# Loading the first head pair's q and k in fp32 by the hardware queues, with the cast on chip

## The chip, the core and the metric

The kernel runs on one core of one Trainium2 chip. A core has five engines with an instruction stream each: TensorE (PE; its weight loads are listed apart as PEld), VectorE (DVE), ScalarE (ACT), GpSimd (POOL) and SyncE (SP). Transfers are issued from an engine's stream: here from POOL, SP and ACT. A transfer issued on POOL can change the type on its way (fp32 in DRAM to bf16 in SBUF); this kernel uses that for nearly all its loads. The metric is the device time of one execution in microseconds, the median over several runs.

## The reference

Two stages. First, an attention with "beacon" keys: 8 batches of 8 heads, 576 queries, and 16 + 576 keys of width 64. Query s may see all 16 beacons and the keys up to its own position:

```
k_all  = concat(beacon_k, k);  v_all = concat(beacon_v, v)
scores = q @ k_all^T / 8, masked causally for the 576 (not for the 16)
a      = softmax(scores);  attn = a @ v_all
```

The heads are then laid side by side into x of 4608 x 512, and a gated feed-forward follows:

```
out = (gelu(x @ w_gate) * (x @ w_val)) @ w_out        # 512 -> 1536 -> 512
```

All inputs and the output are fp32; the kernel computes in bf16 with fp32 sums.

## The kernel before

Per batch, q and k are brought into the form qkT: for each of four head pairs, width along the partitions (two heads of 64), positions along the columns. For the first two batches TensorE does the turning by transposes; later batches use transposing transfers. Scores of a pair are made in four chunks of columns (`CHUNKS`), each an exp on ScalarE into `exp_ring`; for batch 0 the causal mask is added on TensorE, by matmuls of `eye` (a shifted diagonal of ones) with `neg` (a staircase of large negative numbers), in `score_mms`. `attend` multiplies the exps with v, a column of ones gives the sums, `normalize` divides, and the result is turned into xT_sb. `gate_val` and `out_mms` are the feed-forward, run over chunks of 512 tokens and woven in between the attention of the next batch.

The order on each engine is the order in which the program is written: every operation goes through `keep`, which holds it in program order. Nothing is planned by costs. An engine waits only for the data and buffers of its next instruction, and what stands behind a waiting instruction on the same engine waits too.

At the start, which the change is about:

- SP issues the loads of batch 0's beacon keys and values in fp32, `kb_sb` and `vb_sb` (L474 to L477).
- POOL issues, through `load_qk6` (L120), the loads of batch 0's q and k by head pairs, cast to bf16 in flight, into the tile `qk6`: 96 partitions, of which each holds six consecutive positions of every head. Between the third and the fourth load POOL makes `eye` (L480). Loads of v, of the weights and of the next batches follow on the same stream.
- TensorE runs 66 small matmuls on zeros (`warm`, L228 and L519), whose result is not read.
- VectorE casts the two beacon tiles (L520, L521) and makes `neg` from `eye` by a running sum and a scaling (L522, L523).
- `transpose_both(0, 0)` (L223): `transpose_half` for k (12 transposes, and one of the beacon keys), copied out by VectorE (L217); `transpose_half` for q with `by_act`, which first runs eight transposes of zeros as fillers (L209) and then the twelve of q, copied out by ScalarE (L215). `beacon_part` (L221) copies the beacons' 16 columns.
- The first score chunks `c((0, 0))`, `c((0, 2))` follow, then the next pair's transposes, and so on.

Of the kernel before, what the change touches and what calls it, by code (L numbers as in the profile page):

```python
# [7 lines left out]
P = 128  # L8
B, H, S, NB, D = 8, 8, 576, 16, 64
SK = S + NB  # L10
N_TOK = B * S
D_MODEL = 512
# [30 lines left out]
FP32 = mybir.dt.float32  # L43
BF16 = mybir.dt.bfloat16
ACT = mybir.ActivationFunctionType
# [6 lines left out]
def kernel(  # L52
# [12 lines left out]
    nc = tc.nc  # L65
    keep = tc.keep_in_program_order
# [6 lines left out]
    opool = ctx.enter_context(tc.tile_pool(name="opool", bufs=2))  # L73
# [18 lines left out]
    q_ring, k_ring, v_ring = [], [], []  # L92
# [14 lines left out]
    def dma(out_ap, in_ap):  # L107
        keep(nc.gpsimd.dma_start(out=out_ap, in_=in_ap))  # L108

    qk6 = {}  # L110

    def qk6_of(b):
        if b not in qk6:
            qk6[b] = (
                hpool.tile([P, 2, H, 6 * D], BF16, name="qk6", tag="hT_sb"),
                npool.tile([NB, H, D], BF16, name="kb", tag="kb"),
            )
        return qk6[b]

    def load_qk6(b, h0, h1, ws=(1, 0)):  # L120
        for w in ws:
            src = (q, k)[w]
            dma(
                qk6_of(b)[0][0:96, w, h0:h1, :],
                src[b, h0:h1, :, :].rearrange("h (p r) d -> p h (r d)", r=6),
            )
# [44 lines left out]
    def mm(out_ap, lhsT, rhs, start, stop, **kw):  # L171
        keep(nc.tensor.matmul(out_ap, lhsT, rhs, start=start, stop=stop, **kw))  # L172

    def act(out_ap, in_ap, func, **kw):
        keep(nc.scalar.activation(out_ap, in_ap, func, **kw))  # L175
# [30 lines left out]
    def transpose_half(b, m, w, by_act=False):  # L206
        pool, tag = ((psum_o, "o"), (psum_t, "t"))[w]
        t_ps = pool.tile([P, 1024], BF16, name="t_ps", tag=tag)
        for _ in range(8 if by_act else 0):  # L209
            tr(t_ps[0:D, 640:768], idle[:, 0:D])  # L210
        tr_part(b, m, w, t_ps)
        out_ap = qkT[:, m, w, NB:SK].rearrange("p (t r) -> p t r", r=6)
        in_ap = t_ps[:, 0:S].rearrange("p (r t) -> p t r", r=6)
        if by_act:
            act(out_ap, in_ap, ACT.Copy)  # L215
        else:
            keep(nc.vector.tensor_copy(out_ap, in_ap))  # L217
        return t_ps

    def beacon_part(m, t_ps):  # L220
        keep(nc.vector.tensor_copy(qkT[:, m, 1, 0:NB], t_ps[:, S:SK]))  # L221

    def transpose_both(b, m):  # L223
        k_ps = transpose_half(b, m, 1)
        transpose_half(b, m, 0, by_act=m == 0)
        beacon_part(m, k_ps)

    def warm(n):  # L228
        w_ps = psum_s.tile([P, 2, 512], FP32, name="w_ps", tag="s")
        for j in range(n):  # L230
            mm(w_ps[:, 0, 0:D], idle[:, 0:P], idle[:, 0:D], True, True)
# [12 lines left out]
    def scores(b, *parts):  # L244
        s_ps = psum_s.tile([P, 2, 512], FP32, name="s_ps", tag="s")
        c0 = 0
        for m, c in parts:
            score_mms(b, m, c, s_ps[:, :, c0 : c0 + CHUNK_W[c]])
            c0 += CHUNK_W[c]
        (m, c), n = parts[0], len(parts)  # L250
        o, w = CHUNK_OFF[c], CHUNK_W[c]
        act(
            exp_ring[:, m : m + n, :, o : o + w].rearrange("p g h c -> p h g c"),
            s_ps[:, :, 0 : n * w].rearrange("p h (g c) -> p h g c", g=n),
            ACT.Exp,
            scale=QK_SCALE,
        )
        if b:
            for m, c in parts:
                masks(b, m, c)  # L260
# [200 lines left out]
    def out_mms(ci, u0, u1):  # L461
        for u in range(u0, u1):
# [8 lines left out]
                if ci >= N_CHUNKS - 2:  # L471
                    store(nc.sync)

    kb_sb = opool.tile([NB, H, D], FP32, name="kb_sb", tag="o_sb")  # L474
    keep(nc.sync.dma_start(out=kb_sb, in_=beacon_k[0].rearrange("h t d -> t h d")))
    vb_sb = opool.tile([NB, H, D], FP32, name="vb_sb", tag="o_sb")
    keep(nc.sync.dma_start(out=vb_sb, in_=beacon_v[0].rearrange("h t d -> t h d")))  # L477
    load_qk6(0, 0, 2)
    load_qk6(0, 2, 4, (1,))
    keep(  # L480
        nc.gpsimd.affine_select(
            out=eye,
            in_=eye,
# [31 lines left out]
    def c(*parts):  # L515
        scores(0, *parts)

    keep(nc.scalar.preload_act_table_set(SET_EXP))
    warm(66)  # L519
    keep(nc.vector.tensor_copy(qk6[0][1], kb_sb))  # L520
    keep(nc.vector.tensor_copy(v_ring[0][0:NB, 0, :, 0:D], vb_sb))  # L521
    keep(nc.vector.tensor_tensor_scan(neg, eye, idle, -1.0, ALU.add, ALU.add))  # L522
    keep(nc.vector.tensor_scalar_mul(neg, neg, -MASKED))  # L523
    transpose_both(0, 0)
    c((0, 0))
    c((0, 2))
    transpose_both(0, 1)
# [143 lines left out]
```

The softmax here doesn't subtract the row's maximum and nothing guards it: scores larger than these inputs give would overflow.

## Time and profile before

| | |
|---|---|
| Median of 7 runs | 369.71 us (368.66 to 371.42) |
| The profiled execution's own time | 369.48 us |
| Its span, first to last instruction | 367.7 us |
| PE busy | 357.5 us, 97% of the span |
| PEld busy | 183.1 us, 50% |
| DVE busy | 152.3 us, 41% |
| ACT busy | 188.1 us, 51% |
| POOL busy | 161.0 us, 44% |
| Read from HBM, written to it | 38.27 MB, 9.44 MB |
| Transfers issued on POOL (q0) | 104848 packets, 19.11 MB |

Busy shares are means over the whole span; the start, the only part that the change edits, is some 24 us of it. Matmuls are pipelined, so TensorE's 97% is not 97% of its peak. In the views, "out<-in" names the tiles by their names in the program, and the line is that of the helper that records the operation (L172 all matmuls, L180 all transposes, L175 all activations, L108 POOL's loads), so instructions are told apart by their tiles. "SPq", "ACTq" and "POOLq" are the instruction streams that issue transfers. Times in the views are microseconds from the first instruction, if not marked otherwise.

### The profile page before, as it was taken

To read this page: it belongs to the slowest core of one execution; us is meant where nothing else is said; L and a number is where in the kernel's file an instruction comes from. 1 tells how busy PE (TensorE), PEld (TensorE's weight loads), DVE (VectorE), ACT (ScalarE), POOL (GpSimd) and SP (SyncE) were. 2 spreads that over 40 slices of the span, in tenths; PEclk is the share of its full clock that TensorE was granted. 3 is DMA by queue.
4 is the path that set the end of the run, shared out by engine and by line. 5 is a ranking of instruction groups with operands and counts; after the bars stand their busy time and mean duration, and the time that the engine had idled before them with its cause. 6 is when DMAs were issued, how large, how long until landed. Compare 5 with 4: busy or idle time off the path is not lost.

```text
span 367.7 us, 7507 instructions
## 1 busy us (share of the span) xinstructions
PE 357.5 (97%) x3018; PEld 183.1 (50%) x3061; DVE 152.3 (41%) x277; ACT 188.1 (51%) x243; POOL 161.0 (44%) x288
## 2 busy tenths in 40 slices
PE   7899999999999999999999999999999999999996
PEld 7664445444554455444644464445544464444443
DVE  4544536343443335433534254434444253333332
ACT  3963488237923593349623891369334953321210
POOL 8934487484538352954376353836230430000000
PEclk9999999999999999999999999999999999999999
DMA  8999999799259953999399925992495051000112
GB/s 108 176 204 204 194 141 122 134 143 125 79 123 138 136 83 96 146 142 83 69 161 132 136 59 120 150 141 76 108 132 53 33 80 58 0 2 29 57 38 107
DMA packets 154900, 39.65 MB, mean 108 GB/s; under 512 B 141424, under 2 KB 150384, under 8 KB 154864
## 3 DMA queue, kind: packets, MB, share of 16 engines
q0 software_dynamic: 104848, 19.11, 70.1%
q1 hardware_dynamic: 48000, 16.38, 25.7%
q10 hardware_dynamic: 2016, 3.67, 3.2%
q8 instruction: 24, 0.39, 0.4%
q14 instruction: 12, 0.10, 0.1%
HBM read 38.27 MB, written 9.44 MB: 130 GB/s over the span
## 4 chain that ended last, share of the span: by engine, by line
PE 70%; DMA 13%; SPq 7%; DVE 3%; issue 2%; POOL 2%; ACT 0%; POOLq 0%; DVEq 0%
PE gv_ps L172 26%; PE o_ps L172 23%; DMA qkT<-k_sb 9%; PE x_ps L172 9%; PE s_ps L172 8%; SPq L238 6%; DMA q_sb<-in_q_dram 3%; PE t_ps L180 2%; POOL v_sb L108 2%; DMA xT_sb<-y_sb 1%; DVE qkT L217 1%; PE w_ps L172 1%; PE v_ps L172 1%; PE g_ps L172 1%; DVE y_sb L336 1%
## 5 line engine op out<-in xcount | busy, mean ns | idle before, releaser
L175 ACT ACTIVATE ge_sb<-gv_ps 128x512 bf16<-128x512 f32 x101 | 59.5, 597 | 144.7 <-PE gv_ps L172 142.7
L427 DVE TENSOR_TENSOR hT_sb<-gv_ps,ge_sb 128x512 bf16<-128x512 f32 x101 | 69.1, 691 | 115.6 <-ACT ge_sb L175 113.2
L172 PE MATMUL gv_ps<-xT_sb,wg_sb 128*128 128x512 bf16 x394 | 110.9, 379 | 0.5
L172 PE MATMUL gv_ps<-xT_sb,wv_sb 128*128 128x512 bf16 x401 | 110.9, 379 | 0.1
L175 ACT ACTIVATE expT<-s_ps 128x960 bf16<-128x960 f32 (+3 forms) x112 | 99.7, 966 | 8.4 <-PE s_ps L172 8.0
L172 PE MATMUL o_ps<-wo_sb,hT_sb 128*128 128x512 bf16 (+2 forms) x415 | 101.7, 373 | 1.4 <-issue 0.2
L298 POOL TENSOR_SCALAR_AFFINE_SELECT expT<-expT 128x256 bf16<-128x256 bf16 (+2 forms) x140 | 51.8, 387 | 63.8 <-ACT expT L175 60.3
L172 PEld LDWEIGHTS <-wv_sb 128*128 128x128 bf16 x432 | 42.3, 98 | 50.4
L172 PEld LDWEIGHTS <-wg_sb 128*128 128x128 bf16 x432 | 42.0, 98 | 50.5 <-DMA xT_sb<-y_sb 0.7
L172 PEld LDWEIGHTS <-hT_sb 128*128 128x128 bf16 x444 | 38.9, 97 | 42.3 <-DVE y_sb L336 3.1
L172 PEld LDWEIGHTS <-expT 128*128 128x128 bf16 (+1 forms) x960 | 33.5, 97 | 10.8 <-DVE y_sb L336 4.1
L172 PE MATMUL s_ps<-qkT 64*128 64x512 bf16 (+5 forms) x384 | 33.6, 281 | 3.7 <-DVE qkT L221 1.6
L172 PE MATMUL x_ps<-v_sb,expT 128*128 128x65 bf16 (+1 forms) x960 | 37.1, 193 | 0.0
L108 POOL DMA_DIRECT2D v_sb<-in_v_dram x40 | 33.7, 859 | 5.8 <-DMA wv_sb<-in_moe_w_val_dram 1.7
L446 DVE COPY o_sb<-o_ps 128x512 f32<-128x512 f32 (+2 forms) x37 | 25.0, 676 | 27.1 <-PE o_ps L172 26.0
L108 POOL DMA_DIRECT2D k_sb<-in_k_dram x30 | 25.3, 845 | 18.5 <-DMA q_sb<-in_q_dram 13.4
L336 DVE TENSOR_TENSOR y_sb<-x_ps,r_sb 128x320 bf16<-128x320 f32 (+1 forms) x47 | 28.8, 612 | 1.6
L334 DVE RECIPROCAL r_sb<-x_ps 128x5 f32<-128x5 f32 (+1 forms) x47 | 9.6, 204 | 47.0 <-PE x_ps L172 47.0
L108 POOL DMA_DIRECT2D q_sb<-in_q_dram x30 | 25.3, 884 | 3.5 <-DMA wo_sb<-in_moe_w_out_dram 3.5
L172 PEld LDWEIGHTS <-qkT 64*128 64x128 bf16 x384 | 14.4, 94 | 19.7 <-issue 11.2
L378 POOL COPY hold_sb<-xT_sb 128x2 bf16<-128x2 bf16 x6 | 1.1, 187 | 34.7 <-DMA xT_sb<-y_sb 34.7
L613 ACT ACT_TABLE_LOAD x7 | 9.0, 1283 | 0.1
(49 smaller groups left out, 120.0 us busy)
## 6 DMA issues: line engine op xcount, KB each, us to landing
out_dram<-o_sb SPq DMA_DIRECT2D x21, 256.0 KB, 2.4
out_dram<-o_sb ACTq DMA_DIRECT2D x14, 256.0 KB, 3.0
v_sb<-in_v_dram POOLq DMA_DIRECT2D x24, 128.0 KB, 6.3
q_sb<-in_q_dram POOLq DMA_DIRECT2D x24, 128.0 KB, 8.9
k_sb<-in_k_dram POOLq DMA_DIRECT2D x18, 128.0 KB, 7.9
wo_sb<-in_moe_w_out_dram POOLq DMA_DIRECT2D x3, 512.0 KB, 14.4
wg_sb<-in_moe_w_gate_dram POOLq DMA_DIRECT2D x2, 512.0 KB, 11.1
wv_sb<-in_moe_w_val_dram POOLq DMA_DIRECT2D x2, 512.0 KB, 12.8
```

The costliest lines, as they stand in the source:

```text
L108: keep(nc.gpsimd.dma_start(out=out_ap, in_=in_ap))
L172: keep(nc.tensor.matmul(out_ap, lhsT, rhs, start=start, stop=stop, **kw))
L175: keep(nc.scalar.activation(out_ap, in_ap, func, **kw))
L180: keep(nc.tensor.transpose(out_ap, in_ap, ident[0:n, 0:n]))
L217: keep(nc.vector.tensor_copy(out_ap, in_ap))
L238: nc.sync.dma_start_transpose(out=qkT[:, :, w, c + j * P : c + j * P + n], in_=src[0:n, j, :, :].rearrange("p h d -> p (h d)"),)
L298: nc.gpsimd.affine_select(out=d, in_=d, pattern=[[0, 2], [1, n]], compare_op=ALU.is_ge, fill=0.0, base=NB if t == 0 else 0, channel_multip ...
L334: keep(nc.vector.reciprocal(r, x[:, :, :, D:DV]))
L336: nc.vector.tensor_tensor(out=y_of[i][:, :, h0:h1, :].rearrange("p j b d -> p b j d"), in0=x[:, :, :, 0:D], in1=r.to_broadcast([P, h1 - h0 ...
L427: nc.vector.tensor_tensor(out=h_of[ci][:, fi, :], in0=gv_of.pop((ci, fi))[1], in1=ge_sb, op=ALU.mult)
L446: keep(nc.vector.tensor_copy(o_sb[:, ti, c0:c1], o_ps))
L613: keep(nc.scalar.preload_act_table_set(SET_GELU))
```

## The change

Four edits, all at the start of the program.

1. Heads 0 and 1 of q and k for batch 0 no longer come by POOL's casting loads. k is loaded by SP and q by ACT, each as the first transfer of that engine, in fp32, into two tiles `raw` of the pool that later holds the output tiles. The beacon tiles `kb_sb` and `vb_sb` become slices of `raw[1]` that lie beside k; their loads follow k on SP.
2. ScalarE casts k from `raw` into the tile `qk6` (96 x 768, fp32 to bf16), and VectorE casts q.
3. On VectorE `neg` is now made ahead of the casts (of the beacon keys, then of q); the cast of the beacon values moves behind `transpose_both(0, 0)`.
4. `warm` runs 56 matmuls instead of 66.

On POOL the load of k for heads 2 and 3 is now first, and `eye` second.

```diff
-    kb_sb = opool.tile([NB, H, D], FP32, name="kb_sb", tag="o_sb")
+    raw = [opool.tile([P, 4, D_MODEL], FP32, name="raw", tag="o_sb") for _ in range(2)]
+    raw0 = [raw[w][0:96, 0:2, 0 : 6 * D] for w in range(2)]
+    for w, engine in ((1, nc.sync), (0, nc.scalar)):
+        keep(
+            engine.dma_start(
+                out=raw0[w], in_=(q, k)[w][0, 0:2, :, :].rearrange("h (p r) d -> p h (r d)", r=6)
+            )
+        )
+    kb_sb, vb_sb = (raw[1][0:NB, g, :].rearrange("t (h d) -> t h d", h=H) for g in (2, 3))
     keep(nc.sync.dma_start(out=kb_sb, in_=beacon_k[0].rearrange("h t d -> t h d")))
-    vb_sb = opool.tile([NB, H, D], FP32, name="vb_sb", tag="o_sb")
     keep(nc.sync.dma_start(out=vb_sb, in_=beacon_v[0].rearrange("h t d -> t h d")))
-    load_qk6(0, 0, 2)
     load_qk6(0, 2, 4, (1,))
...
     keep(nc.scalar.preload_act_table_set(SET_EXP))
-    warm(66)
-    keep(nc.vector.tensor_copy(qk6[0][1], kb_sb))
-    keep(nc.vector.tensor_copy(v_ring[0][0:NB, 0, :, 0:D], vb_sb))
+    warm(56)
+    act(qk6[0][0][0:96, 1, 0:2, :], raw0[1], ACT.Copy)
     keep(nc.vector.tensor_tensor_scan(neg, eye, idle, -1.0, ALU.add, ALU.add))
     keep(nc.vector.tensor_scalar_mul(neg, neg, -MASKED))
+    keep(nc.vector.tensor_copy(qk6[0][1], kb_sb))
+    keep(nc.vector.tensor_copy(qk6[0][0][0:96, 0, 0:2, :], raw0[0]))
     transpose_both(0, 0)
+    keep(nc.vector.tensor_copy(v_ring[0][0:NB, 0, :, 0:D], vb_sb))
     c((0, 0))
```

## The prediction

> **What bounds the kernel now.** I read the windows view first, cut at the events of the start; its columns are stretch, length, busy us (instructions) of PE, PEld, DVE, ACT and POOL, granted clock, DMA share and GB/s.
>
> ```profile
> 13.07:15.61 2.54, 2.07 (x53) 1.47 (x53) 1.50 (x3) 2.54 (x4) 2.54 (x4) 1.00 2.02 173
> 23.90:367.70 343.80, 337.29 (x2573) 166.61 (x2613) 140.04 (x246) 171.79 (x224) 142.52 (x258) 1.00 0.97 104
> ```
>
> From 23.9 us to the end TensorE is busy 337.29 of 343.80 us, so whatever the change wins or loses must happen ahead of that and then moves the end one for one. The stretch before it is ScalarE's: its exps run without a gap. The timeline has start, duration, engine, line, operation and, in brackets, the idle time before it:
>
> ```profile
> 0.82 0.40 SPq L475 DMA_DIRECT2D kb_sb<-in_beacon_k_dram  x1
> 1.38 0.77 POOL L108 DMA_DIRECT2D qk<-in_k_dram  x1 [0.86 <-POOLq L655]
> 4.76 0.51 PEld L180 LDWEIGHTS <-qk 96*64 96x64 bf16 x12
> 5.39 0.19 PE L180 MATMUL t_ps<-eye,kb 16*128 16x16 bf16 x1
> 5.51 0.80 PE L180 MATMUL t_ps<-eye,idle 128*64 128x128 bf16 x6
> 5.62 0.76 DVE L217 COPY qkT<-t_ps 128x576 bf16<-128x576 bf16 x1 [0.71 <-PE t_ps L180]
> 6.72 0.65 ACT L175 ACTIVATE qkT<-t_ps 128x576 bf16<-128x576 bf16 x1 [4.63 <-PE t_ps L180]
> 7.42 0.39 PE L172 MATMUL s_ps<-qkT 64*128 64x512 bf16 x2 [0.75 <-ACT qkT L175]
> 7.93 6.31 ACT L175 ACTIVATE expT<-s_ps 128x1024 bf16<-128x1024 f32 x7 [0.55 <-PE s_ps L172]
> 8.10 0.31 PEld L180 LDWEIGHTS <-qk 96*64 96x64 bf16 x12
> 13.24 6.12 ACT L175 ACTIVATE expT<-s_ps 128x960 bf16<-128x960 f32 x7
> ```
>
> The exps fill ScalarE from 7.93 to 19.36 us. So the size of the change is the shift of that 7.93. The chain of waits says what leads to it:
>
> ```profile
> 1.13 3.70 PE w_ps L172 x66
> 4.84 1.86 PE t_ps L180 x29
> 6.72 0.66 ACT qkT L175
> 7.42 0.75 PE s_ps L172 x12
> ```
>
> Warm-up, transposes of k and q with eight fillers between, the cast-out of q^T, scores. Nothing here waits for a transfer in the open, as the DMA issues show (KB, us to landing):
>
> ```profile
> qk<-in_k_dram POOLq DMA_DIRECT2D x1, 144.0 KB, 3.3
> qk<-in_q_dram POOLq DMA_DIRECT2D x1, 144.0 KB, 3.2
> kb_sb<-in_beacon_k_dram SPq DMA_DIRECT2D x1, 32.0 KB, 2.0
> out_dram<-o_sb ACTq DMA_DIRECT2D x1, 256.0 KB, 2.0
> ```
>
> k lands at 1.38 + 3.3 = 4.68 us, just under the warm-up's end (4.77); q at 2.14 + 3.2 = 5.34, under the fillers that start at 5.51. The first twelve transposes of k load in 0.51 us, the same twelve of the next pair (8.10) in 0.31: TensorE starts at half clock. In single records the fillers follow each other 107 ns apart up to 6.04 and 56 ns from 6.14, so the clock doubled at about 6.13.
>
> **What the skill says.** (1) "DMA: Bandwidth & Descriptors", section Issuing engines are not separate DMA queues: all issuers share the same 16 engines, and issuing from several saves only issue time. The trace can't yet show two such loads side by side. (2) "TensorE: Matmul & The Clock Gate", Part 1: TensorE doubles its clock after a busy window of about 3.4 us that runs freely. The trace agrees in kind: work from 1.13, full clock at 6.13; the window before that one, had TensorE idle until 1.13 and didn't lift it. How busy is busy enough, neither says.
>
> **The change, part by part.** Its own sum is made against the profiled execution (369.48 us, of it span 367.7, so 1.8 around it); the median shown, 369.71, lies 0.2 higher, and I add that at the end.
>
> *Loads.* k goes out on SP at about 0.82, q on ACT at 0.81, instead of 1.38 and 2.14 on POOL. Each is 2 x 576 x 64 x 4 = 295 kB, 192 runs of 1536 B. An issue holds its queue 0.4 us (row L475). On ACT the table load (0.81, 1.28 us) slips to about 1.2, ending 2.5, before anything needs ScalarE; on SP the beacons slip 0.4. The beacon key's first bytes move at about 1.82, 1.0 us after issue. The 256 KB stores moved at some 360 GB/s (their packets took 0.74 us); that is the nearest row, in the other direction. Both loads start together and, sharing engines, end together: 590 kB / 360 GB/s = 1.6 us, so 3.4; POOL's next load (heads 2 and 3, whose first bytes come near 2.85 because it inherits the slot at 1.38) takes some share: +0.2; from last packet to semaphore about 0.3, as the beacon shows. Landing 3.9 us. Bounds: 2.9 if k were served first, 4.5 if both get half the rate after 2.85. I take 3.9.
>
> *Casts.* k on ScalarE, 96 x 768: rows of 1024 columns take 1049 ns and 832 take 914 on that engine; "ScalarE: Activation LUTs", What ACT_TABLE_LOAD costs, prices an activation at 186 ns + 0.833 ns per column, 826 ns. With semaphores: ready at 3.9 + 0.05 + 0.83 + 0.05 = 4.83. On VectorE the beacon cast is 0.41 us (row L520, 16 x 512). The q cast has 768 columns: 0.41 x 768/512 = 0.62 at most. The beacon key, behind k on SP, lands at about 4.1; cast to 4.55, q to 5.2. VectorE's next work, the copy of k^T, stood at 5.62: covered, with 0.4 to spare; without that cover each 0.1 us late delays k^T, beneath the fillers and q's transposes another 0.3. The q transposes stand behind the fillers, not behind 5.2.
>
> *Mask constants.* Scan 0.69 and scaling 0.23 move ahead of the casts; the diagonal pattern on POOL comes one issue (0.7) after 1.38, at 2.15, so they run 2.6 to 3.6, while VectorE waits for transfers. Their reader is the mask matmul at 7.64. The cast of the beacon values moves behind k^T's small copy, +0.41 on VectorE near 6.5; its next copy is at 8.69 and v is first read at 16.42. All three are nothing on the path.
>
> *POOL.* Two issues leave (0.77 + 0.65): all its later loads start up to 1.4 us earlier. Nothing waits for them: the loads of heads 2 and 3 landed by 7.7 for transposes at 8.1, and no later gap of TensorE ends on a load except 0.2 us once.
>
> *Warm-up.* 56 instead of 66 at 53.5 ns apart: TensorE is free at 4.77 - 0.54 = 4.23 and then waits until 4.83. The wait that the shorter warm-up opens falls on the cast of k: TensorE idles 0.6 us, and everything of the chain is queued behind.
>
> *Sum.* k's transposes start 4.85 against 4.77: +0.08. Fillers begin 5.59; with the clock doubling at 6.13, five go at 107 ns and three at 56, done 6.30 against 6.26: +0.04. From there on the stages are as before. Change 0.0, rounded; span 367.7, profiled time 369.5; with the 0.2, **369.7 us**, own range 369.1 to 370.4 (landing bounds below, and half of the spread of runs).
>
> **Rivals.**
> *A: the loads are quick.* If k lands by 3.3, TensorE goes on at 4.23. For it: the queue is empty before 2.85. But at half clock eight fillers take 0.86 and q's transposes 0.5, so ScalarE's copy starts at 6.53 instead of 6.72: 0.2 gained; were the clock's window to fall elsewhere, at most the 0.54 of the warm-up. 369.2 to 369.5. More than 0.3% (1.1 us) would need the exp stage itself to shrink; it has no gap to give.
> *B, the other side: the hole costs the clock.* Place: 4.23 to 4.85, inside the window from 2.7 to 6.13 that released the clock here. Busy share falls from 100% to 82%. The window before had 46% and wasn't enough; it decides if the threshold lies above 82% (a third of 46 to 100, or surely if transposes count less than matmuls). Price: one window more, to 9.5. Fillers done 6.45, q's transposes 7.15 (before 6.68), first scores 0.27 slower: exps begin 8.65 instead of 7.93, +0.7, and the second pair's transposes, 0.5 more on the way to VectorE's copies: +1.2, time 370.9. A second window adds about 1.1: 372.0.
> *C: the two loads crawl,* landing at 4.5 or beyond. Transposes at 5.45, +0.7 less what the clock gives back: +0.4 to +0.6, 370.2. Against it: the beacon load's 2.0 us shows a short fixed part.
>
> **How the numbers follow.** No change that matters 44%, A 20%, B 22% (near half of it past one window's price), C 10%, and 4% for something faster that I don't see. 0.3% is 1.1 us, about what a measurement of this kernel can tell from no change; the runs before spread from 368.66 to 371.42, which moves some of each case over a bound. Slower: most of B and a little of C, 0.23. Faster: the 4%, and tails of A by spread, 0.11. The rest is 0.66. The range reaches down below A's 369.2 by the spread of a median (0.5), and up over B's first window: 368.7 to 371.5, leaving out a second window and the unseen gain.
>
> **What would show it.** Right: SP's and ACT's issues at 0.8; ScalarE's cast of k starting 3.8 to 4.1 for 0.83; a hole of TensorE of about 0.6 us between w_ps and t_ps; first exp within 0.2 of 7.93; POOL's later issues 1.4 us earlier with no effect on TensorE. A: no hole. B: the second pair's twelve weight loads still take 0.51 us, first exp beyond 8.5. The prediction is wrong if loads issued on SP and ACT interleave differently from what I assume, or if the clock's window reacts to the hole.

## The result: slower by about 1%

The changed kernel took 373.47 us in the median (372.54 to 375.19, 12 runs), the kernel before, run beside it, 369.55 us (367.98 to 372.39, 31 runs). The ratio is 1.0108, with a 95% interval of 1.0091 to 1.0125: about 4.0 us slower, and outside the range of the prediction. The profiled execution took 373.18 us, of it span 371.5.

The windows view of the changed kernel, with the columns as before (stretch, length, busy us and instructions of PE, PEld, DVE, ACT, POOL, granted clock, DMA share, GB/s), cut where the clock records change, and once more at 27.30, 3.4 us behind the last cut of before:

```profile
...
3.83:7.24 3.41, 1.09 (x26) 0.82 (x24) 1.08 (x2) 0.84 (x1) 3.41 (x6) 1.00 1.26 195
7.24:17.48 10.24, 9.32 (x144) 6.60 (x143) 4.14 (x10) 6.54 (x8) 9.58 (x13) 0.50 1.80 179
...
27.30:371.50 344.20, 337.23 (x2573) 166.67 (x2613) 140.05 (x246) 171.82 (x224) 140.63 (x256) 1.00 0.95 102
```

The last row holds the same 2573 matmuls as the row of before from 23.90 us on, and is 344.20 us long instead of 343.80. So 3.4 of the 3.8 us that the span grew lie ahead of it. Two rows show how: from 3.83 to 7.24 TensorE is busy 1.09 of 3.41 us, and from 7.24 to 17.48 it works at half clock. (The clock column reads 1.00 also ahead of a trace's first clock record, so it says nothing of the time before 3.83.)

The chain of waits, start and duration:

```profile
0.82 4.71 DMA raw<-in_k_dram
5.54 0.85 ACT qk L175
6.44 0.45 PE t_ps L180 x12
...
```

Where the warm-up matmuls led to the transposes before, now the load of k does, and its cast. In the timeline, the idle time ahead of the first weight loads of k is the hole:

```profile
1.13 3.01 PE L172 MATMUL w_ps<-idle 128*128 128x64 bf16 x56 [1.13 <-DVE idle L80]
...
5.54 0.84 ACT L175 ACTIVATE qk<-raw 96x768 bf16<-96x768 f32 x1 [2.99 <-DMA raw<-in_k_dram]
...
6.44 0.31 PEld L180 LDWEIGHTS <-qk 96*64 96x64 bf16 x12 [2.41 <-ACT qk L175]
6.44 0.45 PE L180 MATMUL t_ps<-eye,qk 96*64 96x96 bf16 x12 [2.29 <-ACT qk L175]
...
9.91 1.86 ACT L175 ACTIVATE expT<-s_ps 128x1024 bf16<-128x1024 f32 x2 [0.83 <-PE s_ps L172]
...
10.35 0.51 PEld L180 LDWEIGHTS <-qk 96*64 96x64 bf16 x12
```

The first pair's twelve weight loads take 0.31 us and the second pair's, at 10.35, take 0.51: the reverse of before. In the clock records the clock was raised at 3.83 and lost at 7.24. Of the twelve executions six, this one among them, have a mean granted clock of 0.986, which is what three windows of 3.41 us at half clock make of 371.5 us; the others have 0.999 or 1.000. In those the clock was not lost once it had been raised, but a late first rise doesn't show in that figure (e10 below has 1.000 with its clock up at 16.71 us). Exps start at 9.91 instead of 7.93. The transfers from 0.5 to 3.5 us, first the GB/s in 40 equal slices of that stretch, then the issues (KB, us to landing):

```profile
GB/s 0 0 0 0 0 0 0 0 0 0 0 0 0 0 0 0 0 20 102 164 143 102 102 143 61 123 164 164 143 102 205 205 164 307 328 410 369 389 369 389
...
raw<-in_q_dram ACTq DMA_DIRECT2D x1, 288.0 KB, 5.0
raw<-in_k_dram SPq DMA_DIRECT2D x1, 288.0 KB, 4.7
qk<-in_k_dram POOLq DMA_DIRECT2D x2, 144.0 KB, 5.1
```

Both fp32 loads are late, and so are their neighbours: POOL's loads took 3.3 and 3.2 us before, and the beacon keys, 4.9 us here, had taken 2.0. Up to 2.97 us (33 slices of 0.075) no slice moved more than 205 GB/s.

Two suspects stand out, the late k and the lost clock. They come together here, so they had to be pulled apart.

### The profile page after: what moved, and what is told of

It is laid out like the page before. It is cut to its first block, busy times and chain, and to the rows that moved or that the text cites. A ratio compares the mean times of both kernels' runs of the same rounds, so it can differ in the third digit from the quotient of the medians.

```text
span 371.5 us, 7490 instructions
## 1 busy us (share of the span) xinstructions
PE 359.6 (97%) x3008; PEld 184.3 (50%) x3051; DVE 152.9 (41%) x278; ACT 189.1 (51%) x244; POOL 160.3 (43%) x286
## 4 chain that ended last, share of the span: by engine, by line
PE 68%; DMA 20%; POOL 5%; issue 3%; DVE 3%; SPq 0%; ACT 0%; POOLq 0%; DVEq 0%
PE gv_ps L172 26%; PE o_ps L172 21%; PE x_ps L172 9%; DMA qkT<-k_sb 8%; PE s_ps L172 8%; DMA q_sb<-in_q_dram 8%; POOL v_sb L108 4%; DMA xT_sb<-y_sb 3%; PE t_ps L180 2%; DMA raw<-in_k_dram 1%; POOL q_sb L108 1%; DVE qkT L217 1%; PE v_ps L172 1%; PE g_ps L172 1%; DVE y_sb L336 1%
## 5 line engine op out<-in xcount | busy, mean ns | idle before, releaser
L172 PE MATMUL s_ps<-qkT 64*128 64x512 bf16 (+5 forms) x384 | 35.3, 291 | 3.2 <-DMA qkT<-k_sb 0.8
L180 PE MATMUL t_ps<-eye,qk 96*64 96x96 bf16 x192 | 7.9, 232 | 2.3 <-ACT qk L175 2.3
```

Source lines behind the costliest of these rows:

```text
L180: keep(nc.tensor.transpose(out_ap, in_ap, ident[0:n, 0:n]))
```

## Experiments

The theory at the outset: the late landing opens the hole, the hole costs TensorE its clock, and each has a price of its own. Its rivals: only the late start counts, and the clock is a symptom; or only the clock counts. For each run two shifts are given: that of the first gelu on ScalarE (26.07 us before, 29.50 in the changed kernel), behind which TensorE is bound, and that of the median, taken as ratio less 1 times 369.6. Profiles are of one execution each, medians of several: the profiled execution had the longest time of its kernel in e1, e9 and e10 (373.14, 373.83 and 372.71 us) and the shortest in e2 and e11 (371.55 and 368.39), so a shift of the gelu and one of the median needn't agree. "Clock up" is when the trace's clock records show full speed for good; for e1, which has no such record, the weight loads of 6.26 stand in.

### Late without a hole, and a hole without late loads

**e1_warm112**, the changed kernel with a warm-up that covers the late load:

```diff
-    warm(56)
+    warm(112)
```

> The changed kernel with 112 warm-up matmuls instead of 56, so that TensorE has no hole while it waits for k (64 more at 53.5 ns are 3.4 us at half clock, less once the clock is up). Theory 'hole': of the 3.9 us lost, the late landing of k accounts for about 1.2 and the clock, lost in the hole from 4.1 to 6.4 us, for the rest; here the clock should rise once by 8 us and stay, the twelve weight loads of the second pair take 0.31 us, first exp near 9.0, and the time falls to about 370.8 (1.003 of before). Rival 'landing only': half clock is hidden beneath ScalarE's exps, so the loss stays at 3.4 to 3.9 us, 373 to 373.5.

**e2_hole_only**, the kernel before with a warm-up that is too short:

```diff
-    warm(66)
+    warm(24)
```

> The kernel before with 24 warm-up matmuls instead of 66 and nothing else: the loads are as before and k's transposes can still start at 4.7 us, but TensorE idles from about 2.4 to 4.7. Theory 'hole': the clock rises later than 6.13 (9.5 or after), first exp at 8.2 to 8.7, and the time grows by 1 to 2.5 us, 370.6 to 372. Rival 'landing only': warm-up matmuls are read by nobody and the landing is unchanged, so the time is that of before within 0.3 us.

Measured: e1 372.3 us, ratio 1.0055 (1.0029 to 1.0082). e2 371.88 us, 1.0063 (1.0038 to 1.0089). The timeline of e1:

```profile
6.26 0.31 PEld L180 LDWEIGHTS <-qk 96*64 96x64 bf16 x12
...
8.89 2.72 ACT L175 ACTIVATE expT<-s_ps 128x1024 bf16<-128x1024 f32 x3 [0.55 <-PE s_ps L172]
9.06 0.31 PEld L180 LDWEIGHTS <-qk 96*64 96x64 bf16 x12
```

and of e2:

```profile
4.58 0.50 PEld L180 LDWEIGHTS <-qk 96*64 96x64 bf16 x12 [2.15 <-DMA qk<-in_k_dram]
...
8.40 1.86 ACT L175 ACTIVATE expT<-s_ps 128x1024 bf16<-128x1024 f32 x2 [0.83 <-PE s_ps L172]
8.83 0.51 PEld L180 LDWEIGHTS <-qk 96*64 96x64 bf16 x12
```

In e1 the transposes start 1.5 us later than before, nearly as late as in the changed kernel (6.44), but at full clock (0.31 both times). Here k landed after 4.2 us and its cast ended at 5.91, so the last 0.3 us of the delay are the warm-up's own. The median lies 1.5 us above the 370.8 expected. (112 matmuls are 56 more than in the changed kernel, not the 64 of the expectation.) In e2 they start 0.18 us earlier than before, from loads that landed as before, and half clock lasts to 17.52. Either is slower by itself, so neither rival stands. The first gelu moved by 0.96 us in e1, by 2.44 in e2 and by 3.43 in the changed kernel: the two add up (3.40). So do the medians, 0.55% and 0.63% against 1.08%. Up to the gelu the clock is the larger part; by the medians the two are about equal, and their intervals don't decide between these.

**e9_before_warm112** is the other control, late with no new load at all:

```diff
-    warm(66)
+    warm(112)
```

> The kernel before with 112 warm-up matmuls and no fp32 loads: TensorE is busy until 6.2 to 7.1 us though k is there at 4.7, so its turns start as late as in the changed kernel with 112. If that one's end (1.0055 of before, 2 us, while its first gelu is only 0.96 us late) is what such a start costs with any loads, the same comes out here: first gelu about 1 us late, end 1.003 to 1.007. If the fp32 loads cost something further on as well, the end here is nearer to the first gelu: 370.5 to 371, 1.002 to 1.003.

Measured: 372.25 us, 1.0059 (1.0036 to 1.0082), like e1. Transposes at 6.96, clock up at 6.59, the gelu 1.68 us later. A late start costs this with the loads of before too; as far as these intervals go, nothing else about the fp32 loads is needed to explain e1. (The start is 0.7 us later than in e1, so the two are not the same delay.)

### How small a hole is enough

**e3_k_only**: the changed kernel with q brought back to POOL, as its first load.

```diff
-    for w, engine in ((1, nc.sync), (0, nc.scalar)):
+    for w, engine in ((1, nc.sync),):
...
+    load_qk6(0, 0, 2, (0,))
     load_qk6(0, 2, 4, (1,))
...
-    keep(nc.vector.tensor_copy(qk6[0][0][0:96, 0, 0:2, :], raw0[0]))
```

> The changed kernel with q of the first pair back on POOL (cast in flight, POOL's first load); k alone comes by SP in fp32 and is cast by ScalarE. If the two fp32 loads slowed each other (590 kB at once), k lands after about 3.2 us instead of 4.7, at 4.0, and its cast ends at 4.95: hole of 0.8 us. If each such load is slow by itself at this place, k lands at 5.0 or later all the same. Time: between the kernel before and the changed one, 370 to 372 in the first case, 373 in the second.

**e11_k_only_warm72** and **e12_k_only_warm80** are e3 with a longer warm-up:

```diff
-    warm(56)
+    warm(72)        # e12: warm(80)
```

> The changed kernel with q back on POOL and 72 warm-up matmuls, so that k's cast (ready at 5.03 us when k comes alone) meets a TensorE that has just ended them (4.98). The same kernel with 56 had a hole of 0.72 us, a clock that rose only at 16.02, and 1.0047. If the hole cost it the clock, the clock rises by 8 us here and the time falls to 370 to 370.4 (turns 0.26 us later than before, part of it given back by the clock). If fp32 by SP is slow for another reason, it stays near 371.9.

> k alone by SP, q on POOL, with 80 warm-up matmuls instead of 72: they end at 5.41 us if the clock is half all along, up to 0.9 us after k's cast is ready (4.5 to 5.0). With 72 it was 0.9986 of before (0.9959 to 1.0012), two of twelve runs far above the others. If those two lost the clock because it rose early, the warm-up then ran at double speed and left a hole, 80 closes the hole and the tail goes: 0.997 to 0.999. If 72 was long enough, the 0.4 us of later start shows: 1.000 to 1.001.

Measured: e3 371.86 us, 1.0047 (1.0023 to 1.0072); e11 369.31, 0.9986 (0.9959 to 1.0012); e12 369.47, 1.0000 (0.9978 to 1.0021). The timeline of e3:

```profile
5.02 0.50 PEld L180 LDWEIGHTS <-qk 96*64 96x64 bf16 x12 [0.88 <-ACT qk L175]
5.03 0.69 PE L180 MATMUL t_ps<-eye,qk 96*64 96x96 bf16 x12 [0.72 <-ACT qk L175]
...
9.28 0.51 PEld L180 LDWEIGHTS <-qk 96*64 96x64 bf16 x12
```

and of e11:

```profile
1.13 4.02 PE L172 MATMUL w_ps<-idle 128*128 128x64 bf16 x72 [1.13 <-DVE idle L80]
...
5.08 0.31 PEld L180 LDWEIGHTS <-qk 96*64 96x64 bf16 x12
...
7.88 0.31 PEld L180 LDWEIGHTS <-qk 96*64 96x64 bf16 x12
```

The transposes start at the same time, 5.02 and 5.08. What differs is 16 matmuls whose result nobody reads, in a hole of 0.72 us (the matmuls end that much ahead of the transposes). With the hole full clock comes at 16.02 us, without it at 5.10, and the gelu stands at +2.29 against -0.57. This is the plainest proof that an idle TensorE costs the clock here, and it is about the size of hole that the prediction counted on (0.6). Where the clock's windows fell doesn't explain it: the one that decided ended at 5.78 in e3 and at 5.10 in e11, and with either placing e11's work fills the window and e3's hole lies in it. It also answers what the idea is worth: k by SP alone, with a warm-up of 72 or 80 instead of 66 to cover its cast, is no different from the kernel before within what was measured. With 72, two of twelve executions show a mean granted clock of 0.995 and 0.986, and they have the longest times (370.91 and 372.52); with 80, none of fourteen is below 0.999.

**e10_no_fillers** asks the same of the other dummies: the eight fillers between k's and q's transposes go.

```diff
-        for _ in range(8 if by_act else 0):
+        for _ in range(0):
```

> The kernel before without the eight fillers ahead of q's first transposes. q has landed at 5.34, before the fillers start at 5.51, so they can go; TensorE gets to q's transposes 0.7 us earlier if the clock is half at that point, 0.45 if full. Gain 0.4 to 0.7 us, 369.3. Rival: without them TensorE idles longer while ScalarE and VectorE copy, the clock rises later (fillers are part of the busy window up to 6.13), first gelu 1 to 2.4 us late as with the hole, 371 to 372.

Measured: 371.04 us, 1.0026 (1.0007 to 1.0046). Its timeline:

```profile
7.83 1.86 ACT L175 ACTIVATE expT<-s_ps 128x1024 bf16<-128x1024 f32 x2 [0.83 <-PE s_ps L172]
8.27 0.51 PEld L180 LDWEIGHTS <-qk 96*64 96x64 bf16 x12
```

The chain got shorter (q's weight loads at 5.61), and the first exp came 0.1 us earlier than before. Yet the second pair is still at half clock, full speed comes at 16.71, and the gelu is 1.76 us late. Here the gain by a shorter chain lost to the rival, the clock. That is the longest execution of the twenty. Four others took 368.93 to 369.47 us, less than the median of the kernel before beside them (370.02); whether these kept the clock was not traced.

### What the landing takes

**e4_quiet_loads** puts the two fp32 loads, into tiles that nobody reads, late into the kernel before (issued at 335.3 us), where little else moves:

```diff
+    late = [const.tile([P, 2, 6 * D], FP32, name="late", tag=f"late{w}") for w in range(2)]
...
+        if fi == 3:
+            for w in range(2):
+                act(late[w][0:96, 0, 0:2], h_of[N_CHUNKS - 1][0:96, fi, 0:2], ACT.Copy)
+            for w, engine in ((1, nc.sync), (0, nc.scalar)):
+                keep(
+                    engine.dma_start(
+                        out=late[w][0:96],
+                        in_=(q, k)[w][0, 0:2, :, :].rearrange("h (p r) d -> p h (r d)", r=6),
+                    )
+                )
```

> The kernel before with the same two fp32 loads of 288 KB issued together from SP and ACT once more near 320 us, into two tiles that nobody reads, when hardly anything else moves. If 4.7 and 5.0 us to landing is what two such loads cost anywhere, they take 4.5 to 5 here as well. If the slowness belongs to the start of the program, they take about 3.1 (1.0 to the first byte, 590 kB at some 360 GB/s, 0.4 to the semaphore).

**e5_both_on_sp** sends q behind k on SP; **e8_extra_loads** is the kernel before with the two loads added at the start, unread:

```diff
-    for w, engine in ((1, nc.sync), (0, nc.scalar)):     # e5
+    for w, engine in ((1, nc.sync), (0, nc.sync)):
...
+    for w, engine in ((1, nc.sync), (0, nc.scalar)):     # e8, ahead of load_qk6(0, 0, 2)
+        keep(
+            engine.dma_start(
+                out=late[w][0:96],
+                in_=(q, k)[w][0, 0:2, :, :].rearrange("h (p r) d -> p h (r d)", r=6),
+            )
+        )
```

> The changed kernel with q's fp32 load issued on SP behind k's instead of on ACT at the same moment. k alone landed 3.3 us after its issue (with q on POOL), the pair 4.7 and 5.0. If the queue serves its transfers in order, k lands near 3.4 to 3.7 us after issue again and q about 1 us later, while q is needed 1.5 us after k: then the sharing, not fp32, costs the 1.4 us. If the two are served mixed all the same, k lands after 4.5 or more.

> The kernel before, loads and casts unchanged, with the two fp32 loads added on SP (behind the beacons) and ACT into tiles that nobody reads. It shows what they do to POOL's loads: if all share the same engines, POOL's k and q of the first pair land 1 to 1.5 us later than 3.3 and 3.2 us after issue and TensorE's transposes start near 6; if the queues don't hinder each other there, within 0.3 us of before.

Measured: in e4 (370.35 us, one run) the loads of k and q landed 3.7 and 4.3 us after issue: neither of the sizes expected. e5 took 374.67 us and e8 374.37, one run each. The DMA issues of e5:

```profile
raw<-in_k_dram SPq DMA_DIRECT2D x1, 288.0 KB, 3.2
...
raw<-in_beacon_k_dram SPq DMA_DIRECT2D x1, 32.0 KB, 4.3
```

and of e8:

```profile
late<-in_k_dram SPq DMA_DIRECT2D x1, 288.0 KB, 5.4
...
qk<-in_k_dram POOLq DMA_DIRECT2D x1, 144.0 KB, 5.5
```

Three readings. One fp32 load of k takes 2.8 to 3.3 us when no equal stands beside it (e11 2.8, e12 2.9, e3 3.3, e5 3.2). With q's issued at the same moment on ACT it takes 4.7 in the changed kernel and 4.2 in e1; even late in the kernel the pair needs 3.7 and 4.3, and there too the slices are slow at first (at most 258 GB/s up to 337.4 us, then up to 393). And the two hold up their neighbours: in e8, POOL's own k comes 5.5 us after its issue, where it had come after 3.3, and TensorE waits 2.12 us for it although the new loads are read by nobody (gelu +4.86). This agrees with the Trainium skill, "DMA: Bandwidth & Descriptors", section Issuing engines are not separate DMA queues: transfers from different issuers interleave on the same 16 engines.

e5 shows that serving k first doesn't mend it alone. k landed near the forecast and its transposes start at 4.96, behind a hole of 0.66 us, but the beacon keys, now third on SP, came later; their cast ended near 6.8 and the transpose of the beacon keys held TensorE for 1.24 us. Clock up 18.74, gelu +3.95.

### The mask constants, and the holes that were there before

**e6_mask_only**: the kernel before, with VectorE's new order alone.

```diff
-    keep(nc.vector.tensor_copy(qk6[0][1], kb_sb))
-    keep(nc.vector.tensor_copy(v_ring[0][0:NB, 0, :, 0:D], vb_sb))
     keep(nc.vector.tensor_tensor_scan(neg, eye, idle, -1.0, ALU.add, ALU.add))
     keep(nc.vector.tensor_scalar_mul(neg, neg, -MASKED))
+    keep(nc.vector.tensor_copy(qk6[0][1], kb_sb))
     transpose_both(0, 0)
+    keep(nc.vector.tensor_copy(v_ring[0][0:NB, 0, :, 0:D], vb_sb))
```

> The kernel before with only the order of VectorE changed: the mask constants ahead of the cast of the beacon keys, the cast of the beacon values behind the first pair's turns. All theories: the constants need the diagonal pattern at 3.9 us, so the key cast ends at 5.3 and the beacon transpose stands at 5.39: no change, 369.8, ratio 1.000 within 0.002.

Measured: 369.97 us, 1.0002 (0.9981 to 1.0023), gelu +0.05. That part of the change is free.

**e7_fill_holes**: the kernel before with zero matmuls also in the short waits ahead of the first scores of each pair.

```diff
-    def scores(b, *parts):
+    def scores(b, *parts, fill=0):
...
+        for _ in range(fill):
+            mm(s_ps[:, 0, 0:D], idle[:, 0:P], idle[:, 0:D], True, True)
...
-    c((0, 0))
+    c((0, 0), fill=13)       # 13, 7 and 7 for pairs 1, 2 and 3
```

> The kernel before with matmuls on zeros put where TensorE waits in the first 16 us: 13 ahead of the first scores of pairs 0 and 1, 7 ahead of those of pairs 2 and 3, written to the score tile before its first real matmul. Each is at most 53.5 ns, so 13 take 0.70 us of a wait of 0.75, 7 take 0.37 of 0.40. If some runs of the kernel before lose time because the clock rises late or falls back in those waits, their slow tail (up to 371.2) goes and the median falls by 0.2 to 0.6 us. If the clock is safe there anyhow, nothing changes, or up to 0.3 us are lost where a fill runs into its wait.

Measured: 371.2 us, 1.0024 (1.0006 to 1.0043): the hoped-for gain was not there. In its profiled execution the kernel before had its clock from 6.13 on and kept it, so there more filling had nothing to win. In others it may have had: of the 110 executions of the kernel before that ran beside the experiments, 17 have a mean granted clock of 0.995 or less, which is about one window or more at half clock at a place not recorded. Their median is 371.19 us, against 369.73 for the other 93. With the fillings it is one of twenty (372.02 us), and the median is higher all the same. Up to the gelu e7 lost only 0.19 us; the profiled execution lost the rest later, in TensorE's waits of e7 (us, count, longest):

```profile
PE s_ps L172 <- DMA qkT<-k_sb: 1.1, 2, 0.6
PE s_ps L172 <- DMA qkT<-q_sb: 1.1, 1, 1.1
```

### All runs side by side

e4, e5 and e8, one execution each and without a ratio, stand above.

| | clock up | first exp | gelu shift | median shift |
|---|---|---|---|---|
| before | 6.13 | 7.93 | 0 | 0 |
| the change | 17.48 | 9.91 | +3.43 | +4.0 |
| e2: hole, loads as before | 17.52 | 8.40 | +2.44 | +2.3 |
| e3: k alone, hole 0.72 | 16.02 | 8.84 | +2.29 | +1.7 |
| e10: no fillers | 16.71 | 7.83 | +1.76 | +1.0 |
| e9: late, no fp32 loads | 6.59 | 9.59 | +1.68 | +2.2 |
| e1: late, no hole | before 6.3 | 8.89 | +0.96 | +2.0 |
| e7: holes filled | 6.97 | 8.30 | +0.19 | +0.9 |
| e6: mask order alone | 4.29 | 7.69 | +0.05 | +0.1 |
| e12: k alone, warm 80 | 5.58 | 8.16 | -0.12 | 0.0 |
| e11: k alone, warm 72 | 5.10 | 7.71 | -0.57 | -0.5 |

Where the clock came early, the gelu follows the first exp to within 0.4 us; where it came at 16 us or later, the gelu is 1.9 to 2.0 us later than the first exp alone would put it in e2 and e10, and 1.4 to 1.5 in e3 and the changed kernel. The median shift follows the gelu to within 1.1 us, but not better. After the gelu, TensorE waits for the transposing transfers of later batches: 0.2 us in the profile of before, 0.8 in that of the change, but 2.4 in e1, 2.7 in e9 and 2.2 in e7. Since e4, which starts as the kernel before does, shows 1.0 of it, and the profiled executions of e1 and e9 are the longest of theirs, the runs do not tell whether a late start causes it or it varies from execution to execution. About 1 us of e1's median, and 0.7 of e7's, stay open.

## Why the prediction was wrong

**Loads: failed, by size.** The step put both landings at 3.9 us, from the 360 GB/s of the output stores, with 2.9 and 4.5 as bounds. k landed at 5.53, past the upper bound. The rate was not there at the beginning: the slices shown above have at most 205 GB/s from the first bytes to 2.97 us, 307 to 410 from then on. The step reckoned with shared engines but priced the sharing by bytes, at the rate of a store that had the engines to itself (its packets take 0.83 us in the trace, 314 GB/s, instead of the 0.74 read). Loads of that size take some 3 us alone and 3.7 to 5.0 side by side. Another row of before hinted at it, the stores issued between 44 and 60 us, beside other transfers:

```profile
out_dram<-o_sb ACTq DMA_DIRECT2D x2, 256.0 KB, 4.0
```

**Casts: right in length.** ScalarE's cast of k took 0.84 us for a predicted 0.83, and VectorE's of q 0.53 for at most 0.62. The cast of the beacon keys took 0.69 instead of 0.41, behind nothing that mattered in this kernel; e5 shows where it does.

**Mask constants: right**; e6 has the part alone at 1.0002.

**POOL: right in the main.** Its loads were issued earlier and nothing waited for them. The first gained nothing by it: issued 1.39 us earlier, it took 5.6 us instead of 4.1. The next, q of the same heads, landed at 7.29 instead of 7.68.

**Warm-up and Sum: failed, by mechanism.** The step counted a hole of 0.6 us at its length and let the clock rise at 6.13 all the same. The hole was 2.3 us. But even with the landing as forecast it would have failed: e3 has a hole of 0.72 us and transposes at 5.02, close to the forecast's 4.85, and is slower by 0.47%; 16 dummy matmuls in the hole (e11) take all of that away. So the late landing is not the whole error. The likeliest case rested on the sentence that from the doubling on "the stages are as before", and this was false for both holes that were measured, 0.72 and 2.3 us.

**Rival B: right in mechanism and sign; too small and held too unlikely.** It had the clock lost by the hole, the second pair's weight loads at 0.51 us (here at 10.35), and the first exp beyond 8.5 (9.91). Its place holds for e3, whose hole lies in the window from 2.37 to 5.78 and leaves it 79% busy; in the profiled execution of the changed kernel the clock had been raised before the hole. It priced one window more, to 9.5, at 1.2 us, and a second at 1.1. The clock was up for one window and then lost for three, 7.24 to 17.48, since at half clock the exp stage leaves TensorE waiting in between: its windows were 78% and 95% busy, and the clock came back after one of 100%. Its price in e2, hole without late loads, was 2.44 us at the gelu. And the slow landing, C's cause, was held apart as a rival of its own with 370.2: the two add up, and no case had both.

**A** needed a landing by 3.3 us and fell with it; **C** had the landing right, beyond 4.5, but let the clock give back part of it. (A's sum has a slip: its q transposes of 0.5 us would put ScalarE's copy at 6.35. With 0.69, which e10 shows for them at half clock, it comes to about the 6.53 given.)

**The first exp as the measure of the change ("the size of the change is the shift of that 7.93"): right for a late start, not for the clock.** The exps began 1.98 us later, the gelu 3.43: at half clock the scores could not keep up. Up to 20 us ScalarE's exps waited for them three times, at 9.91, 12.62 and 16.23:

```profile
ACT expT L175 <- PE s_ps L172: 2.5, 3, 0.8
```

Before, it was 0.55 us ahead of the first exp, and then none until 19.4. Nor did the rest move one for one, as the first step had it: medians and gelus differ by up to 1.1 us.

## What to carry to other kernels

Dummy matmuls that seem to cover nothing may be what holds TensorE's clock: ask of each new wait in its first microseconds, however short, what it does to the clock window, before asking how long it is. Price a load by its time to landing among the transfers that will start with it, and count what it does to its neighbours' landings; two issues at once are not two loads at the price of one. And when two causes come together, build each alone, because here each cost about half a percent and either could have passed for the whole.

## What the runs showed of the hardware

- Clock windows of 3.41 us are plain in the records, as the Trainium skill has it ("TensorE: Matmul & The Clock Gate", Part 1); the half-clock stretch of the changed kernel, 10.24 us, is three of them. What they count is not busy time alone. Windows with only the warm-up in them raised the clock at a busy share of 79% (the changed kernel) and 93% (e6), and did not at 71%, 64%, 60% and 46% (e7, e4, e9, before). Windows that held the end of the warm-up, a wait and transposes did not raise it at 79% (e3), 81% (e5) and 94% (e10). A window with 32% lost it (the changed kernel).
- With transposes and short score matmuls at half clock, windows that were 78% and 95% busy (the changed kernel) or 90% and 95% (e2) did not raise it; the first one with 100% did. Once full, the clock stayed through windows that were 68% to 78% busy (e4, e6, before, e9). So it is easier to keep than to win back. Part 4 of the same page, on the PE-mode transpose, says that transposes don't count as busy in the same way. The runs neither confirm nor exclude a smaller weight: the 94% of e10, with no score matmul in its window, would fit, but e7's window from 3.56 to 6.97, of which the last 2.2 us are transposes and nothing waits, did raise the clock. What the waits do and what the transposes do is not told apart here.
- The fp32 k landed 1.0 to 1.5 us sooner with q behind it on the same queue (3.2 us, e5) than with q beside it on another (4.7 in the changed kernel, 4.2 in e1); these are single executions.
